# Gate-weight folding in a fused attention, MoE and routed-MoE kernel: weight squares transposed on VectorE, the gate product in pairs of pieces, decode steps in one run

## The chip, the core and the metric

The kernel runs on one core of a Trainium2 chip. The time is device time in microseconds, the median of three runs. TensorE multiplies matrices, VectorE and GpSimd work elementwise, ScalarE does activations and copies, and SyncE (SP) issues the loads. VectorE transposes squares of 32x32 elements within a tile, TensorE whole 128x128 tiles into a PSUM bank.

## What is computed

Three parts follow each other, in fp32: linear attention with random features (2 x 8 heads, 576 rows, 64 wide), a dense expert, and a routed one (top 1 of 8). Cut to what matters:

```python
x = attention(q, k, v, omega)                  # [1152, 512]
h = x @ w_in                                   # [512, 2048], given in float64
y = (h * sigmoid(1.702 * h)) @ w_out           # [2048, 512], given in float64
logits = y @ w_gate                            # [512, 8]
expert = argmax(logits, axis=1)                # each expert has a capacity of 288
out = gate_weight * (relu(y @ w1[expert]) @ w2[expert])   # where the token is kept, else 0
```

For the drawn inputs the kernel needs only half of the tokens' y in full. For the two other groups of tokens it needs the logits alone, and so it multiplies with the product `w_out @ w_gate` (2048 x 8), which it makes on the chip piece by piece.

## The kernel before

**Precision.** A big product is three matmuls in fp32r, a rounded fp32: high times high, high times low, low times high (`mm3`, L82 to L84). So each big operand is held as a high and a low part: ScalarE rounds the high one, VectorE or GpSimd subtracts for the low one.

**Decode.** The two weights `w_in` and `w_out` come as float64 in 16 pieces each, in the order in 0, out 0, in 1, out 1, ..., each 128x512 elements and 512 KB (`wraw`, four buffers). `decode` makes fp32 of one piece in four steps: a, b and c on VectorE by shifts of the two 32-bit words of each number (L220, L223, L226) into a tile `wf` (two buffers), and d, the cast of the high part on ScalarE (L232) and the subtraction of the low part on GpSimd (L233).

**Folding the gate.** For each piece m of `w_out`, three functions make row block m of `w_out @ w_gate`: `do_wt` transposes the four 128x128 squares of `wf` on TensorE (L473) into a PSUM bank and copies it to `wt` on ScalarE (L474). `do_wg` multiplies each by `wg_f`, the gate weights with 8 columns filled up to 32 with zeros (L482), each into its own 32 rows of a bank, copied on ScalarE (L485). `do_wp` transposes that (L490), copies it (L492), and adds the four parts in two steps on GpSimd (L493, L494) into `wp`. An fp32 matmul with a result of 32 rows shows as two instructions in the profile, a transpose as one. These tiles take banks by `mbank`, from two banks, M and L, in turn, or from M alone once the logits hold L.

**Order.** Attention runs in 40 steps, in which loads, transposes, projections, maxima, exponentials and sums are staggered by hand. Six pieces are decoded in it, one each at steps 13, 16, 19, 22, 25 and 28, one decode step of a piece per attention step; rows of q, k and v are asked for ten steps ahead. Then the first expert runs over slots n, listed in `seq`: each is `do_h` of one group G of 288 tokens and one of the 16 column blocks m (12 matmuls), and, for the group and block of two slots before, `do_consume`: for G 0 and 2 `do_y` (12 matmuls), for G 1 and 3 the logit product by `run_lg` (L631), a few blocks together. Groups 0, 1 and 3 run interleaved in rounds, group 2 after them. For G 0 and 2 `do_h` makes g twice on ScalarE (L588, L590) and its low part `glo` on VectorE (L591). The rest of attention is spread over the first slots with priority. The remaining 26 pieces are decoded at about one a slot from slot 0 on, by `decode_slot`: step a in slot n, b half a slot later, c one slot later, d two slots later. `paced` places an instruction behind the last `glo` (mark "v") or the last activation (mark "a") of its engine. The engines run in the order in which the instructions were issued.

**After that** come the positions of the tokens, the load of two experts' weights by a value read on the chip, and two expert passes with `do_h2` and `do_y2`.

Of the kernel before, what the change touches and what calls it, by code (L numbers as in the profile page):

```python
# [15 lines left out]
P = dict(ahead=2, kvlag=2, t2=3, n=5, x=6, dec=(13, 16, 19, 22, 25, 28), tailstep=0.5, zero=26, w0=12, loadlag=10, pv=(0, 4), l1=3, l3=5, db=0.5, hpt=30, dmin=0.9, dc=1, dd=2, dlead=6, dpace=1)  # L16


@with_exitstack
def linear_attention__moe__top1_moe_kernel(  # L20
# [48 lines left out]
    def bank(tag, name):  # L69
        return psA.tile([128, 512], F32, tag=tag, name=name, bufs={"A": 2, "B": 3, "C": 1, "M": 1, "L": 1}[tag])  # L70
# [73 lines left out]
    ps = bank("A", "om_ps")  # L144
# [64 lines left out]
    def decode(kind, m):  # L209

        t = w_raw.pop((kind, m))
        hi, lo = (w_in if kind == "in" else w_out)(m)
        w = t.rearrange("p (n two) -> p n two", two=2)
        low, high = w[:, :, 0], w[:, :, 1]
        f = gp.tile([128, DM], I32, tag="wf", name="wf", bufs=2)
        if kind == "out":
            wfs[m] = f

        def a():
            nc.vector.tensor_scalar(f, high, 3, 0x3FFFFFF8, ALU.logical_shift_left, ALU.bitwise_and)  # L220

        def b():
            nc.vector.scalar_tensor_tensor(f, high, -0x40000000, f, ALU.bitwise_and, ALU.bitwise_or)  # L223

        def c():
            nc.vector.scalar_tensor_tensor(f, low, 29, f, ALU.logical_shift_right, ALU.bitwise_or)  # L226

        def d():
            v = f.bitcast(F32)
            if kind == "in":  # L230
                v = v.rearrange("p (c f) -> p c f", c=KD)
            nc.scalar.copy(hi, v)  # L232
# [21 lines left out]
    def at(s, f):  # L254
        pend.setdefault(s, []).append(f)
# [197 lines left out]
    wg_f = const.tile([128, KD, 32], F32, name="wg_f")  # L453
    wg = const.tile([128, KD, 2, E], F32R, name="wg")
    wp = gate.tile([128, NF, 32], F32, name="wp")
    for t in (wg_f, wp):
        nc.gpsimd.memset(t, 0.0)

    def load_gate():
        nc.sync.dma_start(out=wg_f[:, :, 0:E], in_=moe2_w_gate.rearrange("(c p) e -> p c e", p=128))  # L460
        nc.vector.tensor_copy(wg[:, :, 0], wg_f[:, :, 0:E])
        nc.vector.tensor_tensor(wg[:, :, 1], wg_f[:, :, 0:E], wg[:, :, 0].bitcast(F32), ALU.subtract)


    wts, wws = {}, {}

    def do_wt(m):
        src = wfs.pop(m).bitcast(F32)
        dst = gp.tile([128, DM], F32, tag="wt", name="wt", bufs=1)
        ps = mbank("wt_ps")  # L470
        for c in range(KD):
            dc = slice(c * 128, c * 128 + 128)
            nc.tensor.transpose(ps[:, dc], src[:, dc], ident)  # L473
        nc.scalar.copy(dst, ps)  # L474
        wts[m] = dst

    def do_wg(m):

        t = wts.pop(m)
        ps = mbank("wg_ps")  # L480
        for c in range(KD):
            nc.tensor.matmul(ps[32 * c:32 * c + 32, :128], wg_f[:, c], t[:, c * 128:(c + 1) * 128],  # L482
                             start=True, stop=True)
        t = gp.tile([128, 128], F32, tag="wgt", name="wgt", bufs=1)
        nc.scalar.copy(t, ps[:, :128])  # L485
        wws[m] = t

    def do_wp(m):
        ps = mbank("wp_ps")
        nc.tensor.transpose(ps[:, :128], wws.pop(m), ident)  # L490
        t = gp.tile([128, KD, E], F32, tag="wpt", name="wpt", bufs=1)
        nc.scalar.copy(t, ps[:, :128].rearrange("p (c e) -> p c e", c=KD)[:, :, 0:E])  # L492
        nc.gpsimd.tensor_tensor(t[:, 0:2], t[:, 0:2], t[:, 2:4], ALU.add)  # L493
        nc.gpsimd.tensor_tensor(wp[:, m, 0:E], t[:, 0], t[:, 1], ALU.add)  # L494

    out_t = out.rearrange("(a p) d -> p a d", p=TT)
    zero_at = P["zero"]
# [5 lines left out]
    for s in range(NS + 1):  # L503
        do_T(s + AHEAD)
        if s < NS:
            do_P(s)
        do_Tlo(s + AHEAD)
        if s < NS:
            do_M(s)
        if s:  # L510
            do_E(s - 1)
        if s < NS:
            for f in pend.pop(s, []):
                f()
        if s == P["w0"]:
            load_next(4)
            load_gate()
        if s in DEC_AT:
            fs = decode_next(1)
            for d in range(4):  # L520
                at(s + d + 1, fs[d])
            at(s + 4, load_next)
            kd, m = wseq[wl[1] - 1]
            if kd == "out":
                at(s + 4, lambda m=m: do_wt(m))
                at(s + 6, lambda m=m: do_wg(m))
                at(s + 8, lambda m=m: do_wp(m))
# [43 lines left out]
    def slot(n, f):  # L571
        side.setdefault(round(n * 2) / 2, []).append(f)
# [497 lines left out]
```

## Time and profile before

| | us |
|---|---|
| median of 3 runs (lowest, highest) | 346.32 (346.31, 347.48) |
| profiled execution | 345.72 |
| its span, first to last instruction | 343.9 |
| TensorE busy, matmuls / weight loads | 323.6 / 303.6 |
| VectorE busy | 195.1 |
| ScalarE busy | 174.2 |
| GpSimd busy | 67.8 |

The busy time of TensorE counts pipelined matmuls whose ends are modelled, so that a full engine is not one at its peak. PE is TensorE's matmul, PEld its weight load, DVE VectorE, ACT ScalarE, POOL GpSimd, and SPq the queue on which SyncE issues loads. A row of a group gives the busy time and the mean duration, behind the bar the idle time just before these instructions and what ended it.

### The profile page before, as it was taken

The page shows a single profiled execution, that of the slowest core. Times are in us where ns is not written, and L with a number is a line of the kernel's source. Part 1 is how long each engine was busy: PE and PEld are TensorE (multiplying, and loading weights), DVE is VectorE, ACT ScalarE, POOL GpSimd, SP SyncE. Part 2 cuts the span into 40 slices and gives each one's busy share as a digit, 9 for nine tenths or more (in the row PEclk, how much of TensorE's full clock was granted, in tenths as well). Part 3 has the DMA queues.
Part 4 walks back from the last instruction along what each step waited for, and adds up shares of the span by engine and source line. Part 5 has one row for each costly group of instructions (what it writes and reads, how often), then busy time and mean ns, then how long its engine had stood idle before and what let it go on. Part 6 is the DMA issues. An engine that isn't in the chain of part 4 may idle for free.

```text
span 343.9 us, 6686 instructions
## 1 busy us (share of the span) xinstructions
PE 323.6 (94%) x2569; PEld 303.6 (88%) x2569; DVE 195.1 (57%) x438; ACT 174.2 (51%) x453; POOL 67.8 (20%) x99
## 2 busy tenths in 40 slices
PE   5899999999998999989899999999999999999991
PEld 4799988898887888888789998989999999999990
DVE  6577797896588445999992002316444132668322
ACT  3698898888864444454543123234344133175312
POOL 4110312130031565475753000000000001010000
PEclk9999999999999999999999999999999999999996
DMA  5999332310032453555510000251320000293202
GB/s 166 297 342 269 140 132 65 121 62 2 0 124 64 153 195 97 170 182 163 168 40 0 2 2 1 79 167 41 116 91 0 2 0 3 67 309 115 71 1 77
DMA packets 29079, 35.19 MB, mean 102 GB/s; under 512 B 5360, under 2 KB 23792, under 8 KB 29040
## 3 DMA queue, kind: packets, MB, share of 16 engines
q1 hardware_dynamic: 29040, 34.69, 31.2%
q8 instruction: 22, 0.36, 0.4%
q14 instruction: 17, 0.14, 0.1%
HBM read 32.33 MB, written 2.36 MB: 101 GB/s over the span
## 4 chain that ended last, share of the span: by engine, by line
PE 71%; DVE 10%; ACT 6%; DMA 5%; issue 4%; SPq 2%; POOL 1%; ACTq 0%; DVEq 0%
PE h_ps L82 10%; PE h_ps L84 10%; PE h_ps L83 10%; PE y L82 6%; PE y L84 6%; PE y L83 6%; PE nps L348 4%; PE kvp L323 4%; DVE wf L226 3%; DMA eraw<-in_moe_w_dram 3%; DVE x_lo L383 3%; PE wt_ps L473 2%; PE t L337 2%; ACT x_hi L382 2%; PE pj L83 2%
## 5 line engine op out<-in xcount | busy, mean ns | idle before, releaser
L591 DVE TENSOR_TENSOR glo<-g,ghi 128x288 fp32r<-128x288 f32 x32 | 15.7, 491 | 59.0 <-ACT g L590 58.9
L226 DVE SCALAR_TENSOR_TENSOR wf<-wraw,wf 128x512 int32<-128x512 int32 x32 | 36.1, 1128 | 0.7
L588 ACT ACTIVATE ghi<-h_ps 128x288 fp32r<-128x288 f32 x32 | 13.1, 410 | 42.1 <-PE h_ps L84 42.1
L583 ACT ACTIVATE g<-h_ps 128x288 f32<-128x288 f32 x32 | 13.2, 411 | 31.9 <-PE h_ps L84 27.0
L292 DVE TENSOR_REDUCE nb<-pj 128x4 f32<-128x512 f32 (+1 forms) x40 | 24.9, 628 | 3.5 <-PE pj L84 3.4
L810 DVE TENSOR_TENSOR el<-eraw,eh 128x1024 fp32r<-128x1024 f32 x16 | 19.5, 1223 | 11.0 <-ACT eh L809 10.9
L880 POOL MEMSET base<- 96x1536 f32 x2 | 2.8, 1378 | 113.4 <-PE h_ps L84 113.4
L82 PE MATMUL pj<-om_hi,xh 128*128 128x256 f32 x72 | 23.9, 332 | 1.1 <-ACT qp L305 1.1
L223 DVE SCALAR_TENSOR_TENSOR wf<-wraw,wf 128x512 int32<-128x512 int32 x32 | 23.0, 718 | 0.4
L809 ACT CAST eh<-eraw 128x1024 fp32r<-128x1024 f32 x16 | 16.7, 1050 | 12.4 <-PE h_ps L83 7.4
L305 ACT ACTIVATE qp<-pj,nb 128x128 f32<-128x128 f32 x72 | 21.7, 384 | 1.3 <-DVE nb L292 1.1
L305 ACT ACTIVATE kp<-pj,nb 128x128 f32<-128x128 f32 x72 | 21.3, 386 | 0.1
L83 PE MATMUL pj<-om_lo,xh 128*128 128x256 f32 x72 | 21.1, 293 | 0.0
L84 PE MATMUL pj<-om_hi,xl 128*128 128x256 f32 x72 | 21.1, 293 | 0.0
L82 PE MATMUL h_ps<-x_hi,win1h 128*128 128x288 f32 x64 | 20.4, 318 | 0.0
L220 DVE TENSOR_SCALAR wf<-wraw 128x512 int32<-128x512 int32 x32 | 15.7, 492 | 8.2 <-POOL wout1l L233 5.0
L323 PE MATMUL kvp<-vt,kp 128*128 128x65 f32 (+1 forms) x144 | 20.3, 270 | 0.0
L269 ACT CAST xh<-tp 128x256 fp32r<-128x256 f32 (+1 forms) x40 | 14.5, 363 | 11.3 <-PE tp L266 11.2
L82 PE MATMUL h_ps<-x_hi,win0h 128*128 128x288 f32 x64 | 20.1, 313 | 0.0
L82 PE MATMUL h_ps<-x_hi,win2h 128*128 128x288 f32 x64 | 19.9, 311 | 0.0
L84 PE MATMUL h_ps<-x_hi,win0l 128*128 128x288 f32 x64 | 19.5, 305 | 0.0
L276 DVE TENSOR_TENSOR xl<-tp,xh 128x256 fp32r<-128x256 f32 (+1 forms) x40 | 15.6, 392 | 6.7 <-ACT xh L269 6.4
(212 smaller groups left out, 1108.6 us busy)
## 6 DMA issues: line engine op xcount, KB each, us to landing
wraw<-in_moe_w_in_dram SPq DMA_DIRECT2D x16, 512.0 KB, 3.6
wraw<-in_moe_w_out_dram SPq DMA_DIRECT2D x16, 512.0 KB, 3.5
eraw<-in_moe_w_dram SPq DMA_DIRECT2D x16, 512.0 KB, 4.4
qk_raw<-in_v_dram SPq DMA_DIRECT2D x4, 512.0 KB, 5.2
qk_raw<-in_q_dram SPq DMA_DIRECT2D x4, 512.0 KB, 5.3
qk_raw<-in_k_dram SPq DMA_DIRECT2D x3, 512.0 KB, 5.1
out_dram<-zer SPq DMA_DIRECT2D x2, 576.0 KB, 4.9
out_dram<-base SPq DMA_DIRECT2D x6, 192.0 KB, 2.9
```

The lines of the kernel that those rows point to most:

```text
L82: nc.tensor.matmul(o, lh, rh, start=start, stop=False)
L83: nc.tensor.matmul(o, lh, rl, start=False, stop=False)
L84: nc.tensor.matmul(o, ll, rh, start=False, stop=stop)
L220: nc.vector.tensor_scalar(f, high, 3, 0x3FFFFFF8, ALU.logical_shift_left, ALU.bitwise_and)
L223: nc.vector.scalar_tensor_tensor(f, high, -0x40000000, f, ALU.bitwise_and, ALU.bitwise_or)
L226: nc.vector.scalar_tensor_tensor(f, low, 29, f, ALU.logical_shift_right, ALU.bitwise_or)
L292: mark["M", s] = nc.vector.tensor_reduce(nb[:, :nj], pj[:, :nj * M].rearrange("p (a m) -> p a m", m=M), AX, ALU.min)
L305: nc.scalar.activation(t[:, i], pj[:, i * M:(i + 1) * M], ACTF.Exp, bias=nb[:, i:i + 1], scale=-1.0)
L323: nc.tensor.matmul(ps[:, o:o + n], kp[:, i], vts[p][:, u, c0:c0 + n], start=(f == 0), stop=(f == NU - 1))
L591: mark["v"] = nc.vector.tensor_tensor(glo, g32, ghi.bitcast(F32), ALU.subtract)
L809: nc.scalar.copy(hi, tv)
L810: nc.vector.tensor_tensor(lo, tv, hi.bitcast(F32), ALU.subtract)
```

## The change

- `do_wt` transposes a piece in 16 squares of 32x32 per 32 partitions, with one instruction on VectorE, into one half of a tile `wt` for two pieces; no PSUM bank, no copy.
- `do_wg` runs once for two pieces (odd m). The stationary side is `wgd`: for each of the 16 blocks of 32 gate rows a 128x32 matrix whose four diagonal blocks are the same 32x8 weights, zeros elsewhere. 16 matmuls of 64 columns, in four groups of result rows, add up over four blocks each; one copy of 128x64.
- `do_wp` runs once for two pieces: eight matmuls of 8 columns with `fold32`, four unit matrices of 32 below each other, transpose and add the parts in one; one copy of 128x16 writes `wp` of both. The additions on GpSimd go.
- `wgd` is loaded by four more loads of the gate weights in 32-byte runs, into a tile that GpSimd filled with zeros.
- Step c of decode writes its result in place into the low words of the raw tile. `wf` has one buffer; cast, subtraction and transpose read every second word of the raw tile.
- In `decode_slot` a, b, c and the transpose are all placed in slot n; the products come at n + 2 and n + 3, for odd m only.
- `wp` has 8 columns instead of 32. `run_lg` writes 8 rows instead of 32 of each part of its bank, which VectorE sets to zero first, once.

```diff
-        f = gp.tile([128, DM], I32, tag="wf", name="wf", bufs=2)
+        f = gp.tile([128, DM], I32, tag="wf", name="wf", bufs=1)
         if kind == "out":
-            wfs[m] = f
+            wfs[m] = low.bitcast(F32)
...
         def c():
-            nc.vector.scalar_tensor_tensor(f, low, 29, f, ALU.logical_shift_right, ALU.bitwise_or)
+            nc.vector.scalar_tensor_tensor(low, low, 29, f, ALU.logical_shift_right, ALU.bitwise_or)
 
         def d():
-            v = f.bitcast(F32)
+            v = low.bitcast(F32)
...
+    NB = DM // 32
+    wg_f = const.tile([128, KD, E], F32, name="wg_f")
+    wp = gate.tile([128, NF, E], F32, name="wp")
+    wgd = const.tile([128, NB, 4 * E], F32, name="wgd")
+    nc.gpsimd.memset(wgd, 0.0)
+    fold32 = const.tile([128, 32], F32, name="fold32")
+    nc.gpsimd.tensor_tensor(fold32, ident[:, 0:32], ident[:, 32:64], ALU.add)
+    for i in (64, 96):
+        nc.gpsimd.tensor_tensor(fold32, fold32, ident[:, i:i + 32], ALU.add)
 
     def load_gate():
+        nc.sync.dma_start(out=wg_f, in_=moe2_w_gate.rearrange("(c p) e -> p c e", p=128))
+        for a in range(4):
+            nc.sync.dma_start(out=wgd[32 * a:32 * a + 32, :, a * E:(a + 1) * E],
+                              in_=moe2_w_gate.rearrange("(b i) e -> i b e", i=32))
...
     def do_wt(m):
-        src = wfs.pop(m).bitcast(F32)
-        dst = gp.tile([128, DM], F32, tag="wt", name="wt", bufs=1)
-        ps = mbank("wt_ps")
-        for c in range(KD):
-            dc = slice(c * 128, c * 128 + 128)
-            nc.tensor.transpose(ps[:, dc], src[:, dc], ident)
-        nc.scalar.copy(dst, ps)
-        wts[m] = dst
+        if m % 2 == 0:
+            wts[m // 2] = gp.tile([128, NB, 2, 32], F32, tag="wt", name="wt", bufs=1)
+        nc.vector.transpose(wts[m // 2][:, :, m % 2], wfs.pop(m).rearrange("p (b j) -> p b j", j=32))
 
     def do_wg(m):
-        t = wts.pop(m)
+        t = wts.pop(m // 2)
         ps = mbank("wg_ps")
-        for c in range(KD):
-            nc.tensor.matmul(ps[32 * c:32 * c + 32, :128], wg_f[:, c], t[:, c * 128:(c + 1) * 128],
-                             start=True, stop=True)
-        t = gp.tile([128, 128], F32, tag="wgt", name="wgt", bufs=1)
-        nc.scalar.copy(t, ps[:, :128])
-        wws[m] = t
+        for x in range(NB // 4):
+            for c in range(4):
+                nc.tensor.matmul(ps[32 * c:32 * c + 32, :64], wgd[:, 4 * x + c],
+                                 t[:, 4 * x + c].rearrange("p m j -> p (m j)"),
+                                 start=(x == 0), stop=(x == NB // 4 - 1))
+        wus[m] = gp.tile([128, 2, 32], F32, tag="wgt", name="wgt", bufs=1)
+        nc.scalar.copy(wus[m].rearrange("p m j -> p (m j)"), ps[:, :64])
 
     def do_wp(m):
+        t = wus.pop(m)
         ps = mbank("wp_ps")
-        nc.tensor.transpose(ps[:, :128], wws.pop(m), ident)
-        t = gp.tile([128, KD, E], F32, tag="wpt", name="wpt", bufs=1)
-        nc.scalar.copy(t, ps[:, :128].rearrange("p (c e) -> p c e", c=KD)[:, :, 0:E])
-        nc.gpsimd.tensor_tensor(t[:, 0:2], t[:, 0:2], t[:, 2:4], ALU.add)
-        nc.gpsimd.tensor_tensor(wp[:, m, 0:E], t[:, 0], t[:, 1], ALU.add)
+        for i in range(2):
+            for a in range(4):
+                nc.tensor.matmul(ps[32 * a:32 * a + 32, i * E:(i + 1) * E], t[:, i], fold32[:, a * E:(a + 1) * E],
+                                 start=True, stop=True)
+        nc.scalar.copy(wp[:, m - 1:m + 1].rearrange("p m e -> p (m e)"), ps[:, :2 * E])
...
     def run_lg():
         if not held:
             held.append(bank("L", "lgt_ps"))
+            nc.vector.memset(held[0][:, :GS], 0.0)
...
     def decode_slot(n):
         fs = decode_next(1)
-        paced(fs[0], "v")()
-        slot(n + P["db"], paced(fs[1], "v"))
-        slot(n + P["dc"], paced(fs[2], "v"))
+        kd, m = wseq[wl[1] - 1]
+        for f in fs[:3]:
+            paced(f, "v")()
+        if kd == "out":
+            paced(lambda: do_wt(m), "v")()
         slot(n + P["dd"], paced(fs[3], "a"))
         slot(n + P["dd"], load_next)
-        if kd == "out":
-            slot(n + P["dd"], lambda: do_wt(m))
-            slot(n + P["dd"] + 1, lambda: do_wg(m))
-            slot(n + P["dd"] + 2, lambda: do_wp(m))
+        if kd == "out" and m % 2:
+            slot(n + P["wgl"], lambda: do_wg(m))
+            slot(n + P["wgl"] + 1, lambda: do_wp(m))
```

## Rows read from the trace of the kernel before

**Rows 1.** View by stretches: length, busy us (x instructions) of each engine, clock, DMA.

```profile
0.00:86.00 86.00, 78.47 (x659) 73.65 (x659) 65.10 (x170) 68.61 (x218) 17.46 (x45) 1.00 0.51 159
86.00:132.00 46.00, 43.17 (x344) 39.16 (x343) 28.79 (x65) 25.12 (x59) 14.95 (x15) 1.00 0.31 104
132.00:184.00 52.00, 49.85 (x416) 44.51 (x416) 45.92 (x56) 25.88 (x64) 31.94 (x34) 1.00 0.41 132
```

**Rows 2.** View of waits, 86 to 132 us: us in total, times, longest.

```profile
PEld wt_ps L473 <- PE wp_ps L490: 1.2, 2, 0.6
```

**Rows 3.** View of waits, 132 to 184 us.

```profile
PEld wt_ps L473 <- ACT wpt L492: 3.9, 8, 1.0
...
PE wt_ps L473 <- DVE wf L226: 1.5, 2, 0.8
```

**Rows 4.** Timeline of TensorE around the three groups: start, us, instructions.

```profile
128.40 0.29 PE L84 MATMUL y<-ghi,wout1l 128*128 128x288 f32 x1
128.62 0.43 PE L482 MATMUL wg_ps<-wt,wg_f 128*32 128x128 f32 x8
...
129.21 0.29 PE L83 MATMUL h_ps<-x_lo,win1h 128*128 128x288 f32 x1
...
156.96 0.30 PE L84 MATMUL h_ps<-x_hi,win2l 128*128 128x288 f32 x1
157.09 0.27 PE L490 MATMUL wp_ps<-ident,wgt 128*128 128x128 f32 x1
...
157.34 0.29 PE L83 MATMUL h_ps<-x_lo,win1h 128*128 128x288 f32 x1
...
157.87 0.29 PE L84 MATMUL h_ps<-x_hi,win1l 128*128 128x288 f32 x1
158.13 0.66 PE L473 MATMUL wt_ps<-ident,wf 128*128 128x128 f32 x4
...
158.76 0.29 PE L83 MATMUL h_ps<-x_lo,win1h 128*128 128x288 f32 x1
...
159.52 0.69 PE L631 MATMUL lgt_ps<-g,wp 128*32 128x288 f32 x8
160.03 0.40 PE L482 MATMUL wg_ps<-wt,wg_f 128*32 128x128 f32 x8
```

**Rows 5.** View by stretches, 146 to 182 us.

```profile
146.00:182.00 36.00, 34.05 (x286) 30.20 (x285) 33.88 (x39) 18.08 (x47) 22.80 (x24) 1.00 0.41 132
```

**Rows 6.** Groups of VectorE's instructions, 146 to 182 us.

```profile
L226 DVE SCALAR_TENSOR_TENSOR wf<-wraw,wf 128x512 int32<-128x512 int32 x12 | 20.3, 1690 | 0.4
L223 DVE SCALAR_TENSOR_TENSOR wf<-wraw,wf 128x512 int32<-128x512 int32 x12 | 8.3, 694 | 0.3
L220 DVE TENSOR_SCALAR wf<-wraw 128x512 int32<-128x512 int32 x11 | 4.7, 423 | 0.0
L591 DVE TENSOR_TENSOR glo<-g,ghi 128x288 fp32r<-128x288 f32 x4 | 1.8, 458 | 1.3 <-ACT g L590 1.3
```

**Rows 7.** Groups by line and shape, whole span.

```profile
L292 DVE TENSOR_REDUCE nb<-pj 128x4 f32<-128x512 f32 x32 | 21.7, 681 | 1.5 <-PE pj L84 1.4
...
L588 ACT ACTIVATE ghi<-h_ps 128x288 fp32r<-128x288 f32 x32 | 13.1, 410 | 42.1 <-PE h_ps L84 42.1
...
L474 ACT COPY wt<-wt_ps 128x512 f32<-128x512 f32 x16 | 9.4, 589 | 5.2 <-PE wt_ps L473 5.0
...
L383 DVE TENSOR_TENSOR x_lo<-xps,x_hi 128x512 fp32r<-128x512 f32 x8 | 8.7, 1093 | 5.9 <-ACT x_hi L382 5.9
```

**Rows 8.** Timeline of all engines, GpSimd's subtraction and VectorE's step c.

```profile
152.51 1.50 POOL L233 TENSOR_TENSOR wout2l<-wf,wout2h 128x512 fp32r<-128x512 f32 x1 [0.31 <-ACT wout2h L232]
...
152.90 1.67 DVE L226 SCALAR_TENSOR_TENSOR wf<-wraw,wf 128x512 int32<-128x512 int32 x1
```

**Rows 9.** View of the tile wg_f: its load's issue (ns) and its landing.

```profile
L460 SPq DMA_DIRECT2D wg_f<-in_moe_w_gate_dram x1: 378/378/378, 19.9 to 19.9; - x1
...
DMA to landing us min/median/max: 7.3/7.3/7.3
```

More of the change, by code (lines that the diff above doesn't have):

```diff
@@ L15 @@
 AX = mybir.AxisListType.X
-P = dict(ahead=2, kvlag=2, t2=3, n=5, x=6, dec=(13, 16, 19, 22, 25, 28), tailstep=0.5, zero=26, w0=12, loadlag=10, pv=(0, 4), l1=3, l3=5, db=0.5, hpt=30, dmin=0.9, dc=1, dd=2, dlead=6, dpace=1)
+P = dict(ahead=2, kvlag=2, t2=3, n=5, x=6, dec=(13, 16, 19, 22, 25, 28), tailstep=0.5, zero=26, w0=12, loadlag=10, pv=(0, 4), l1=3, l3=5, wgl=2, hpt=30, dmin=0.9, dc=1, dd=2, dlead=6, dpace=1)
 @with_exitstack
@@ L450, in paced @@
         return g
-    wg_f = const.tile([128, KD, 32], F32, name="wg_f")
+    NB = DM // 32
+    wg_f = const.tile([128, KD, E], F32, name="wg_f")
     wg = const.tile([128, KD, 2, E], F32R, name="wg")
-    wp = gate.tile([128, NF, 32], F32, name="wp")
-    for t in (wg_f, wp):
-        nc.gpsimd.memset(t, 0.0)
-    def load_gate():
-        nc.sync.dma_start(out=wg_f[:, :, 0:E], in_=moe2_w_gate.rearrange("(c p) e -> p c e", p=128))
-        nc.vector.tensor_copy(wg[:, :, 0], wg_f[:, :, 0:E])
-        nc.vector.tensor_tensor(wg[:, :, 1], wg_f[:, :, 0:E], wg[:, :, 0].bitcast(F32), ALU.subtract)
@@ L465, in linear_attention__moe__top1_moe_kernel @@
-    wts, wws = {}, {}
-    def do_wt(m):
-        src = wfs.pop(m).bitcast(F32)
-        dst = gp.tile([128, DM], F32, tag="wt", name="wt", bufs=1)
-        ps = mbank("wt_ps")
-        for c in range(KD):
-            dc = slice(c * 128, c * 128 + 128)
-            nc.tensor.transpose(ps[:, dc], src[:, dc], ident)
-        nc.scalar.copy(dst, ps)
-        wts[m] = dst
+    wp = gate.tile([128, NF, E], F32, name="wp")
+    wgd = const.tile([128, NB, 4 * E], F32, name="wgd")
+    nc.gpsimd.memset(wgd, 0.0)
@@ new lines, in linear_attention__moe__top1_moe_kernel @@
+    fold32 = const.tile([128, 32], F32, name="fold32")
+    nc.gpsimd.tensor_tensor(fold32, ident[:, 0:32], ident[:, 32:64], ALU.add)
+    for i in (64, 96):
+        nc.gpsimd.tensor_tensor(fold32, fold32, ident[:, i:i + 32], ALU.add)
+    def load_gate():
+        nc.sync.dma_start(out=wg_f, in_=moe2_w_gate.rearrange("(c p) e -> p c e", p=128))
+        for a in range(4):
+            nc.sync.dma_start(out=wgd[32 * a:32 * a + 32, :, a * E:(a + 1) * E],
+                              in_=moe2_w_gate.rearrange("(b i) e -> i b e", i=32))
+        nc.vector.tensor_copy(wg[:, :, 0], wg_f)
+        nc.vector.tensor_tensor(wg[:, :, 1], wg_f, wg[:, :, 0].bitcast(F32), ALU.subtract)
@@ L477, in do_wg @@
+    wts, wus = {}, {}
+    def do_wt(m):
+        if m % 2 == 0:
+            wts[m // 2] = gp.tile([128, NB, 2, 32], F32, tag="wt", name="wt", bufs=1)
+        nc.vector.transpose(wts[m // 2][:, :, m % 2], wfs.pop(m).rearrange("p (b j) -> p b j", j=32))
     def do_wg(m):
-        t = wts.pop(m)
+        t = wts.pop(m // 2)
         ps = mbank("wg_ps")
-        for c in range(KD):
-            nc.tensor.matmul(ps[32 * c:32 * c + 32, :128], wg_f[:, c], t[:, c * 128:(c + 1) * 128],
-                             start=True, stop=True)
@@ L525, in linear_attention__moe__top1_moe_kernel @@
                 at(s + 4, lambda m=m: do_wt(m))
-                at(s + 6, lambda m=m: do_wg(m))
-                at(s + 8, lambda m=m: do_wp(m))
+                if m % 2:
+                    at(s + 6, lambda m=m: do_wg(m))
+                    at(s + 8, lambda m=m: do_wp(m))
         if s == zero_at:
@@ L629, in run_lg @@
             held.append(bank("L", "lgt_ps"))
+            nc.vector.memset(held[0][:, :GS], 0.0)
         for i, (m, g) in sorted(lgq.items()):
-            nc.tensor.matmul(held[0][32 * i:32 * i + 32, :GS], wp[:, m], g, start=(m < 2), stop=(m >= NF - 2))
+            nc.tensor.matmul(held[0][32 * i:32 * i + E, :GS], wp[:, m], g, start=(m < 2), stop=(m >= NF - 2))
         lgq.clear()
@@ L894, in decode_slot @@
         assert fs
-        paced(fs[0], "v")()
-        slot(n + P["db"], paced(fs[1], "v"))
-        slot(n + P["dc"], paced(fs[2], "v"))
+        kd, m = wseq[wl[1] - 1]
[3 more added lines that the diff above has]
+            paced(lambda: do_wt(m), "v")()
         slot(n + P["dd"], paced(fs[3], "a"))
         slot(n + P["dd"], load_next)
-        kd, m = wseq[wl[1] - 1]
-        if kd == "out":
-            slot(n + P["dd"], lambda: do_wt(m))
-            slot(n + P["dd"] + 1, lambda: do_wg(m))
-            slot(n + P["dd"] + 2, lambda: do_wp(m))
+        if kd == "out" and m % 2:
+            slot(n + P["wgl"], lambda: do_wg(m))
+            slot(n + P["wgl"] + 1, lambda: do_wp(m))
     for i, (kd, m) in enumerate(wseq[npre:]):
```

## The prediction

> **What bounds the kernel now.** I cut the span into three stretches by what the lines do: attention (0 to 86 us), the first expert rounds with the attention tail in them (86 to 132), and the rounds in which decode still runs (132 to 184); after 184 no line that the diff touches runs any more, except the logit products of L631. The view by stretch [rows 1] shows TensorE as the fullest engine everywhere: 78.5 of 86, 43.2 of 46 and 49.9 of 52 us. VectorE comes close only in the third stretch, 45.9 of 52. The granted clock is 1.00, the upper level of 2.4 GHz, in all three, so no gain or loss comes from the clock. So the question is first what leaves TensorE, and second what VectorE, nearly full in the third stretch, does with more work.
>
> The waits by stretch show what else ends there: between 132 and 184 its weight loads stood still ahead of the transposes of L473 eight times, 3.9 us, until a copy had freed the one PSUM bank [rows 3]; between 86 and 132 twice, 1.2 us [rows 2].
>
> **TensorE, what goes.** The pitch of two matmuls is 0.13 us [rows 4], from 156.96 to 157.09. From the L84 before a group to the second matmul behind it would be two pitches, 0.27 us. Measured so, one piece m costs: the last transpose 157.34 - 156.96 - 0.27 = 0.11 us; the four transposes of L473 158.76 - 157.87 - 0.27 = 0.62, of which 0.13 is the wait ahead of them (they start two pitches after L84 instead of one), so 0.50; the eight instructions of L482 129.21 - 128.40 - 0.27 = 0.54. Together 1.15 us, and 2.30 us for two pieces.
>
> **TensorE, what comes.** Each fp32 matmul with a 32-row result is two instructions (L482 shows eight for four matmuls). So a pair's gate product is 32 instructions and its folding 16, in steps of four that share the array by column groups. The 0.54 us of L482 hold two steps and the change of the array's layout there and back. What a further step of 64 or 8 columns costs no row shows. From below: eight instructions of 288 columns take 160.03 - 159.52 = 0.51 us, 0.25 a step, and 64 columns in proportion 0.06. From above: L482's 0.54, with the first 0.22 (128.40 to 128.62, one pitch of it normal) taken off, leaves 0.45 for two steps and the way back; I let a step be no more than 0.15. I take 0.10, between the two, since the loading of the stationary side doesn't shrink with the columns. Then the product is 0.54 + 6 x 0.10 = 1.14 us and the folding 0.54 + 2 x 0.10 = 0.74, 1.88 us a pair (1.56 to 2.28). A pair saves 0.42 us (0.02 to 0.74). Eight pairs: 3.4 us (0.2 to 5.9).
>
> By stretch, with three pieces and one pair in attention, four pieces and two pairs to 132, nine pieces and five pairs to 184: 3 x 1.15 - 1.88 = 1.6 us, 4 x 1.15 - 2 x 1.88 = 0.8 us, 9 x 1.15 - 5 x 1.88 = 1.0 us.
>
> **The waits for the bank.** With no L473 its waits go. Each hides one normal pitch: 1.2 - 2 x 0.13 = 0.9 us in the second stretch, 3.9 - 8 x 0.13 = 2.9 us in the third. The wait for the last decode step (1.5 us, twice [rows 3]) lies partly inside the same gaps; I add 0.3. What is late next: the products of a pair wait for VectorE's square transposes two slots after decode, and these are not in TensorE's way before that.
>
> **ScalarE and GpSimd.** The 128x512 copy of 0.59 us a piece [rows 7] goes, and both small additions on GpSimd. Neither engine sets the end after 86 us (ScalarE 25.1 of 46 and 25.9 of 52); in attention ScalarE is busy 68.6 of 86, so I count attention's 1.6 us of TensorE as 1.2, between nothing (if VectorE's added 3 x 0.68 us are what ends there) and 2.5 (if ScalarE's 3 x 0.59 and more count on top).
>
> **VectorE.** What each slot's decode costs there in its busiest part: from 146 to 182 us it is busy 33.88 of 36 us [rows 5] with twelve pieces and four glo [rows 6], 33.88 / 12 = 2.82 us a slot. L226 shows 1.69 us where L223, the same kind of operation, takes 0.69: the pair of rows in [rows 8] shows why, L226 stands next to GpSimd's subtraction and ends half a microsecond behind it. So VectorE and GpSimd exclude each other for about 1.0 us a piece.
>
> The new transpose of 128x512 in 32x32 squares has no row. From below: L220, the fastest operation on 128x512, 0.42 us. From above: L383, 128x512 with a PSUM operand, 1.09, or, if it is shut out by GpSimd as L226 is, 1.69. I take L292's 0.68 [rows 7], one input of 512 elements, as this has. The Trainium skill (Vector Engine (DVE) Microarchitecture Reference, section 3.8) says that the reorder array keeps one element per cycle and lane, which at 0.96 GHz is an estimate of 0.53 us without the fixed part; by it the slot below is 0.07 us shorter. No run here shows it yet.
>
> One transpose in two slots: 2.82 + 0.34 = 3.16 us a slot. The rule that bears on it in the Trainium skill (SBUF — State Buffer, section SBUF: two separate sides) is that GpSimd and an instruction of VectorE with two SBUF inputs lock each other out whole; [rows 8] agrees with its 1.67 us. By that rule a transpose, with one input, could run beside GpSimd, and the slot would fall to something between 2.82 and 3.16.
>
> Against that TensorE's slot: the 52 us of the third stretch less 1.0 and 3.2 us is 47.8 us in 17 slots, 2.8 us. VectorE may fall behind: what is queued behind a, b, c and the transpose is the next glo, and the y products want glo two slots after it is made. So 15 slots of VectorE have the time of 17 of TensorE: it decides from 17 x 2.8 / 15 = 3.18 us a slot on, and each 0.1 us above costs 1.5 us. My 3.16 stands just under it; I take 0.5 us of new wait.
>
> The single wf buffer and the in-place third step take away VectorE's waits for GpSimd, which cost nothing but the wait already counted. The raw buffer is held until cast, subtraction and transpose are done; four buffers and a slot of 2.8 us leave 11 us for what takes about 3 us and a load, so nothing. A transpose of an even piece waits until the products of the pair before have read the one wt buffer; these come in the same slot, so under 1 us, while VectorE isn't ahead.
>
> Two more costs I take as nothing. ScalarE's cast and GpSimd's subtraction now read every second word; L220 and L226 read so already at the prices shown, and for the other two engines no row says it; a fifth more of GpSimd's 1.50 us [rows 8] would be 0.3 us a slot, more than the price of the second rival below. And a, b and c in one piece, 1.8 us, can stand ahead of the attention tail's normalising in the second stretch: once or twice, so 0 to 2 us, and since those steps are given priority I take none.
>
> **The logit bank.** It is now cleared by VectorE, once, before the first logit product; no row shows a clearing of 288 columns; from above it is glo's 0.46 us [rows 6], two inputs of that size, from below nothing, and I take 0.3. In program order it comes behind glo of the same slot, which waits for two activations (0.41 each [rows 7]) of the h that TensorE has just done; TensorE stands for 2 x 0.41 + 0.46 + 0.3 = 1.6 us, once. If the instructions are put in another order, nothing. I take 1.6.
>
> **Loads.** Four more loads of the gate weights, in 32-byte runs. The one before took 0.38 us on the SP queue and 7.3 us to land [rows 9]. Four more issues are 1.5 us, and what is queued behind them are the rows of a later part of attention, asked for ten steps ahead; 86 us over 40 steps make that 20 us. Even four landings that follow each other at the time of one issue each stay inside that. Cost 0 to 1.5 us; I take 0.
>
> **Sum.** Attention -1.2; second stretch -0.8 - 0.9 = -1.7; third -1.0 - 3.2 + 0.5 = -3.7; logit bank +1.6: -5.0 us. The profiled execution took 345.7 us (span 343.9), the runs' median is 346.3, 0.6 above. So 345.7 - 5.0 + 0.6 = 341.3; I say 341.3 us.
>
> **Rivals.**
> *VectorE becomes the pacer.* If a transpose is locked out like L226 and takes 1.69 us, a slot is 2.82 + 0.85 = 3.67 us, 0.49 over the point of 3.18: 15 x 0.49 = 7.4 us instead of the 0.5 counted, 348.2 us, slower than before. For it: VectorE is busy 45.9 of 52 us there, and that GpSimd shuts it out is plain in [rows 8]. Against it: only two-input operations show the 1.69 in [rows 6]; L220 with one input stands at 0.42. Slower by 0.5% needs about 3.66 us a slot. 12 in 100.
> *The wait only changes its name.* With 1.09 us a transpose the slot is 3.37, and 15 x 0.19 = 2.9 us come back as waits of y for glo: 343.7 us. For it: VectorE was nearly full before. 20 in 100 (343 to 346).
> *The narrow products are dear.* At 0.15 us a step a pair costs 2.28 us and the 3.4 us are gone: 344.5 us, only the waits are won. For it: many more instructions, 48 a pair against 26. 13 in 100 (343 to 346).
> *All goes well:* steps of 0.06 us (2.5 us more), no stand for the clearing (1.6), attention in full (1.3): 335.9 us. 8 in 100.
> The forecast itself, 338.5 to 343.5, has the other 47.
>
> **How the numbers follow.** About 0.5%, 1.7 us, is what a measurement of this kernel can tell from no change; slower begins at 348.0, faster ends at 344.6. Faster: the forecast, the lucky case, and most of the second and third rivals, 47 + 8 + 21 = 76. The same: 12 from these two and 1 from the first, 13. Slower: the rest of the first, 11. The range of 8 in 10 leaves out the lucky end and the slow end: 336 to 346.8.
>
> **What would show it.** The profile after should have four-instruction steps of L482's successor 0.06 to 0.15 us apart, transposes on VectorE of 0.6 to 0.75 us, no wait for wt_ps, and TensorE busy over 51 of 52 us in the third stretch. A transpose above 1.0 us, or waits of y for glo there of more than 2 us, would prove the VectorE step wrong; a gap at the first logit product shows the clearing. The prediction fails most easily in the 3.16 against 3.18.

## The result and the profile after

The changed kernel takes 351.0 us (350.1 to 351.6, four runs) against 346.9 us (346.3 to 348.1, four runs): ratio 1.013, 95% interval [1.010, 1.015]. It is slower by 1.3% where 341.3 us were forecast. The profiled execution took 351.04 us, its span is 349.3.

The same view by stretches as [rows 1], with one stretch more (length, busy us and instructions of PE, PEld, DVE, ACT and POOL, clock, DMA share, GB/s), of the changed kernel:

```profile
0.00:86.00 86.00, 76.73 (x660) 71.79 (x661) 67.65 (x169) 64.85 (x207) 16.52 (x41) 1.00 0.54 160
86.00:132.00 46.00, 44.54 (x436) 41.09 (x436) 39.11 (x78) 24.21 (x58) 13.62 (x9) 1.00 0.33 98
132.00:184.00 52.00, 44.83 (x448) 41.00 (x447) 49.13 (x59) 18.17 (x45) 23.24 (x16) 0.93 0.44 138
184.00:230.00 46.00, 45.09 (x376) 42.08 (x378) 7.53 (x32) 11.92 (x31) 1.32 (x1) 0.96 0.10 31
```

The third stretch has turned over. TensorE had 49.85 of 52 us and now has 44.83; VectorE had 45.92 and now has 49.13; and the granted clock, 1.00 before, is 0.93. ScalarE lost 7.7 us of work there and GpSimd 8.7, and the time did not fall by it. In the second stretch VectorE went from 28.79 us to 39.11; run e2 below shows where that comes from. What TensorE waits for from 86 to 190 us (us in total, times, longest):

```profile
PE wg_ps L488 <- DVE wt L481: 7.8, 4, 2.8
...
PE y L83 <- DVE glo L599: 0.3, 1, 0.3
```

So the wait sits where the gate product of a pair wants the squares that VectorE transposes (L481), and not, as the prediction had it, where y wants glo. The timeline of TensorE shows the gate products (L488) with the idle time before them:

```profile
131.22 0.65 PE L488 MATMUL wg_ps<-wt,wgd 128*32 128x64 f32 x32
...
144.92 0.92 PE L488 MATMUL wg_ps<-wt,wgd 128*32 128x64 f32 x32 [2.03 <-DVE wt L481]
...
158.49 0.84 PE L488 MATMUL wg_ps<-wt,wgd 128*32 128x64 f32 x32 [2.80 <-DVE wt L481]
...
170.53 0.65 PE L488 MATMUL wg_ps<-wt,wgd 128*32 128x64 f32 x32 [0.80 <-DVE wt L481]
...
184.91 0.65 PE L488 MATMUL wg_ps<-wt,wgd 128*32 128x64 f32 x32 [2.12 <-DVE wt L481]
```

From the pair at 131.22, for which the view names no wait, to the last it is (184.91 - 131.22) / 4 = 13.42 us a pair. VectorE's timeline has the same beat: nine transposes from 130.36 to 184.05, 6.71 us apart in the mean, with two decode slots in each:

```profile
130.36 0.71 DVE L481 STREAM_TRANSPOSE wt<-wraw 128x512 f32<-128x512 f32 x1
...
184.05 0.71 DVE L481 STREAM_TRANSPOSE wt<-wraw 128x512 f32<-128x512 f32 x1
```

VectorE needs 3.36 us a slot and gives TensorE its beat. Between those two transposes it is busy 50.75 of 53.69 us, 3.17 us a slot, and the view of waits names nothing that it waits for; the other 0.18 us a slot are small gaps between its instructions:

```profile
130.36:184.05 53.69, 46.38 (x486) 42.26 (x485) 50.75 (x62) 19.00 (x46) 23.24 (x16) 0.94 0.44 138
```

One round in the timeline of VectorE, the shortest (5.62 us, with one step drawn out by GpSimd and no glo):

```profile
144.06 0.71 DVE L481 STREAM_TRANSPOSE wt<-wraw 128x512 f32<-128x512 f32 x1
144.70 0.38 DVE L220 TENSOR_SCALAR wf<-wraw 128x512 int32<-128x512 int32 x1
145.12 1.68 DVE L223 SCALAR_TENSOR_TENSOR wf<-wraw,wf 128x512 int32<-128x512 int32 x1
146.90 0.69 DVE L226 SCALAR_TENSOR_TENSOR wraw<-wraw,wf 128x512 int32<-128x512 int32 x1
147.62 0.43 DVE L220 TENSOR_SCALAR wf<-wraw 128x512 int32<-128x512 int32 x1
148.09 0.69 DVE L223 SCALAR_TENSOR_TENSOR wf<-wraw,wf 128x512 int32<-128x512 int32 x1
148.88 0.69 DVE L226 SCALAR_TENSOR_TENSOR wraw<-wraw,wf 128x512 int32<-128x512 int32 x1
149.68 0.71 DVE L481 STREAM_TRANSPOSE wt<-wraw 128x512 f32<-128x512 f32 x1
```

The groups of VectorE's instructions from 132 to 184 us, to set beside [rows 6]:

```profile
L226 DVE SCALAR_TENSOR_TENSOR wraw<-wraw,wf 128x512 int32<-128x512 int32 x16 | 17.9, 1121 | 1.7
L223 DVE SCALAR_TENSOR_TENSOR wf<-wraw,wf 128x512 int32<-128x512 int32 x16 | 15.0, 939 | 0.6
L220 DVE TENSOR_SCALAR wf<-wraw 128x512 int32<-128x512 int32 x15 | 10.0, 667 | 0.2
L481 DVE STREAM_TRANSPOSE wt<-wraw 128x512 f32<-128x512 f32 x7 | 5.0, 711 | 0.5
```

The time that GpSimd's subtraction takes from VectorE no longer falls on L226 above all: L220, L223 and L226 are hit by turns. Their sum, 0.67 + 0.94 + 1.12 = 2.73 us, is nearly that of before (0.42 + 0.75 + 1.52 = 2.69 in the same stretch).

As a mark for the whole I use the start of the one copy of the gathered logits. It was at 230.8 us and is now at 234.7, 3.9 us later, and nothing behind it has to do with the change: from it to the end of the span are 113.1 us before, 114.6 in the changed kernel, and 113.4 to 114.7 in the runs below that leave the logits as they are.

### The profile page after: what moved, and what is told of

Its sections match the earlier page's. It is cut to its first block, busy times and chain, and to the rows that moved or that the text cites. A ratio compares the mean times of both kernels' runs of the same rounds, so it can differ in the third digit from the quotient of the medians.

```text
span 349.3 us, 7032 instructions
## 1 busy us (share of the span) xinstructions
PE 321.5 (92%) x2745; PEld 303.1 (87%) x2745; DVE 211.7 (61%) x455; ACT 162.2 (46%) x421; POOL 57.5 (16%) x69
## 4 chain that ended last, share of the span: by engine, by line
PE 59%; DVE 25%; ACT 4%; DMA 4%; issue 3%; SPq 2%; DVEq 0%; ACTq 0%
PE h_ps L82 8%; PE h_ps L83 8%; PE h_ps L84 8%; DVE wraw L226 7%; DVE wf L223 6%; PE y L82 5%; PE y L83 5%; PE y L84 5%; DVE wf L220 5%; PE nps L348 4%; PE kvp L323 4%; DMA eraw<-in_moe_w_dram 3%; DVE wt L481 2%; PE t L337 2%; DVE x_lo L383 2%
## 5 line engine op out<-in xcount | busy, mean ns | idle before, releaser
L599 DVE TENSOR_TENSOR glo<-g,ghi 128x288 fp32r<-128x288 f32 x32 | 14.8, 462 | 52.8 <-ACT g L598 52.8
L226 DVE SCALAR_TENSOR_TENSOR wraw<-wraw,wf 128x512 int32<-128x512 int32 x32 | 31.7, 990 | 2.3
L223 DVE SCALAR_TENSOR_TENSOR wf<-wraw,wf 128x512 int32<-128x512 int32 x32 | 26.6, 832 | 0.8
L220 DVE TENSOR_SCALAR wf<-wraw 128x512 int32<-128x512 int32 x32 | 22.2, 693 | 0.7 <-DMA wraw<-in_moe_w_in_dram 0.4
L305 ACT ACTIVATE kp<-pj,nb 128x128 f32<-128x128 f32 x72 | 21.3, 383 | 0.0
L82 PE MATMUL y<-hhi,eh 128*128 128x288 f32 x64 | 19.1, 298 | 0.9 <-DVE z L850 0.9
L323 PEld LDWEIGHTS kvp<-vt,kp 128*128 128x128 f32 x144 | 19.0, 191 | 0.8 <-issue 0.3
L83 PE MATMUL h_ps<-x_lo,win2h 128*128 128x288 f32 x64 | 19.7, 308 | 0.0
```

The source lines that it names most:

```text
L82: nc.tensor.matmul(o, lh, rh, start=start, stop=False)
L83: nc.tensor.matmul(o, lh, rl, start=False, stop=False)
L226: nc.vector.scalar_tensor_tensor(low, low, 29, f, ALU.logical_shift_right, ALU.bitwise_or)
L305: nc.scalar.activation(t[:, i], pj[:, i * M:(i + 1) * M], ACTF.Exp, bias=nb[:, i:i + 1], scale=-1.0)
L323: nc.tensor.matmul(ps[:, o:o + n], kp[:, i], vts[p][:, u, c0:c0 + n], start=(f == 0), stop=(f == NU - 1))
L599: mark["v"] = nc.vector.tensor_tensor(glo, g32, ghi.bitcast(F32), ALU.subtract)
```

## The experiments

Three theories stood: A, VectorE has become the pacer and TensorE waits for it; B, decode in one run, in place and with one wf tile costs; C, the products merely stand too early, two slots behind decode.

**e1_narrow.** The changed kernel; from piece 4 on the transpose takes one of 16 blocks, and one tile wt stays throughout:

```diff
...
-            wts[m // 2] = gp.tile([128, NB, 2, 32], F32, tag="wt", name="wt", bufs=1)
-        nc.vector.transpose(wts[m // 2][:, :, m % 2], ...)
...
+        wts[m // 2] = st_wt[0]
+        k = NB if m < 4 else 1
+        nc.vector.transpose(st_wt[0][:, :k, m % 2], ...[:, :k])
```

> From piece 4 on the kernel transposes only one of the 16 column blocks of each w_out piece (the rest of the tile keeps older values), so 15/16 of the square transposes are left out; all else stands as in the changed kernel. Theory A (VectorE's added transposes, 0.71 us each, make it the pacer of decode, TensorE then waits for them ahead of the gate products and its clock falls in those gaps): twelve times about 0.6 us of VectorE leave, the 7.8 us of waits ahead of the gate products nearly vanish, the clock of the third stretch is 1.00 again, 340 to 344 us. Theory B (decode in one run with one wf buffer and in-place step c costs the time): 349 to 351 us, waits unchanged. Theory C (the products stand too early, two slots behind decode, and that alone makes TensorE wait): waits fall by a third at most, 347 to 350 us.

A miss, by its own flaw: the waits for wt grew to 15.8 us, five times, while VectorE was busy only 36.1 of 52 us from 132 to 184. With one tile that stays, the next even transpose stands ahead of the products in program order, and these wait for it too (a transpose at 123.02 us, the products at 123.29). The logits also send more tokens on, so the whole time (563.7 us) says nothing.

**e2_decode.** The kernel before, with the decode part of the change alone: wf with one buffer, step c in place, a, b and c in one slot.

```diff
-        slot(n + P["db"], paced(fs[1], "v"))
-        slot(n + P["dc"], paced(fs[2], "v"))
+        for f in fs[:3]:
+            paced(f, "v")()
```

> The kernel before with the decode part of the change alone: one wf buffer, step c in place in the raw tile, a, b and c in one slot; transposes and gate products stay on TensorE as before. Theory A: VectorE's work is that of before, 344 to 347.5 us, clock 1.00 in the third stretch. Theory B: 349 to 351 us, most of the loss is here already. Theory C: 344 to 347.5 us.

345.7 us, ratio 0.997 [0.995, 0.999]; from 132 to 184 us TensorE is busy 50.32 of 52 us at clock 1.00. B falls. The run also shows what filled VectorE from 86 to 132 us: it is busy 38.37 of 46 us here, without one square transpose. Before, step a waited 7.0 us in that stretch for GpSimd to free a `wf`; without these waits the steps meet GpSimd's subtractions (b takes 1.02 us in the mean, 0.68 before). What had been waiting became drawn-out steps, at no cost in time.

**e3_late4.** The changed kernel with the products four slots behind decode (`wgl=2` becomes `wgl=4`).

> The changed kernel with the gate products two slots later (four behind decode instead of two). Theory A: VectorE's total is unchanged, so the wait moves to other places (the next even piece's transpose waits for the one wt buffer, y waits for glo), 348 to 353 us. Theory B: 349 to 352 us. Theory C: the wait ahead of the gate products vanishes, 342 to 346 us.

346.0 us, 0.998 [0.995, 1.001]. What TensorE waits for from 86 to 190 us:

```profile
PE y L83 <- DVE glo L599: 3.5, 4, 2.3
PE lgt_ps L640 <- DVE lgt_ps L638: 2.0, 1, 2.0
```

A's range is missed, and C's upper edge is met. The place of the products is worth 5 us of 351.0 (two more slots of distance would be 2 x 2.56 = 5.1, an estimate from e4's slot below), but VectorE is as full as in the change (49.55 of 52 us), TensorE's waits now stand ahead of y and of the first logit product, and VectorE's beat is nearly the same, (184.52 - 144.88) / 3 = 13.21 us a pair:

```profile
144.88 0.71 DVE L481 STREAM_TRANSPOSE wt<-wraw 128x512 f32<-128x512 f32 x1
...
184.52 0.71 DVE L481 STREAM_TRANSPOSE wt<-wraw 128x512 f32<-128x512 f32 x1
```

Both theories hold a part: VectorE sets the beat, and the place says who feels it first, and how soon.

**e4_pace15.** The changed kernel, with the slot of decode i set at 1.5 i instead of i, as far as the due time allows:

```diff
-dpace=1
+dpace=1.5
```

The line that uses it is `n = max(int(i * P["dmin"]), min(need, int(i * P["dpace"])))`.

> The changed kernel with the remaining decodes at 1.5 slots a piece instead of one, bounded by when the weights are needed. Theory A: VectorE has 1.5 slots (about 4 us) for some 3.4 us of work a piece and is the pacer no longer; waits ahead of the products below 2 us, clock 1.00, 340 to 344 us. Theory B: decode costs the same wherever it stands, 348 to 351 us. Theory C: the products still stand two slots behind decode, but the transposes are then on time, so about as in A.

337.5 us, 0.975 [0.970, 0.980]: 13.5 us faster than the change as it was, and faster than the kernel before. The view by stretches, 132 to 230 us:

```profile
132.00:184.00 52.00, 52.00 (x530) 47.89 (x529) 46.69 (x58) 19.57 (x49) 20.99 (x14) 1.00 0.44 136
184.00:230.00 46.00, 46.00 (x392) 42.18 (x391) 15.64 (x49) 15.23 (x38) 4.30 (x3) 1.00 0.13 47
```

TensorE never stands still there, the clock is 1.00, no wait for wt is left, and the logits are copied at 221.8 us. The same instructions, spread over more slots, are the whole difference: what was lost is a matter of the rate at which VectorE is asked for work, and not of TensorE's cost of the new products.

**e5_narrow2.** e1 mended: the tiles turn over as in the change, and the products read the one block that is transposed.

> The changed kernel, where from piece 4 on only one of the 16 column blocks of each w_out piece is transposed and the gate products read that one block sixteen times; 15/16 of the square transposes are left out and the logits of two groups come out wrong, so extra expert passes run at the end and only the part up to the copy of the logits (at 234.7 us in the changed kernel, 230.8 before) is compared. Theory A (the added transposes make VectorE the pacer): the copy comes at 222 to 227 us, waits ahead of the gate products below 2 us, clock of the third stretch 1.00. Theory B (decode in one run and in place): 233 us or later. The run before this one, with one tile kept for all pairs, let the products read behind the next pair's transpose, which is why its waits grew; here the tiles turn over as in the changed kernel.

The small transposes take 0.21 us and the logits are copied at 228.2 us, 6.5 earlier than in the change, where 222 to 227 was named for A: the direction is right, the size short. VectorE still waits out a, b, c and GpSimd's subtraction (busy 45.40 of 52), and 4.4 us of waits for wt remain. Eight transposes shorter by 0.5 us would be 4.0 of the 6.5 us; where the other 2.5 come from was not followed. The whole time (645.5 us) has more expert passes, as in e1.

**e6_double.** Each transpose is made twice, one behind the other.

> The changed kernel with every square transpose done twice. Theory A: 13 to 16 more transposes of 0.71 us, most of them on the path: 358 to 363 us. Theory that only the place of the products counts: 351 to 354 us. If VectorE had slack: 351 us.

355.7 us, 1.026 [1.022, 1.029]; waits for wt 12.1 us (5 times), logits copied at 240.7, 6.0 later. The time is 4.7 us above the change: 2.3 below the range named for A, 1.7 above the one for the place of the products alone, and well above the 351 of a VectorE with slack. Eight more transposes after the pair at 131 us would be 8 x 0.71 = 5.7 us, but that this comes near 6.0 is luck. VectorE's timeline has the last transposes of that pair and of the last one at

```profile
132.39 1.46 DVE L483 STREAM_TRANSPOSE wt<-wraw 128x512 f32<-128x512 f32 x2
...
188.15 1.46 DVE L483 STREAM_TRANSPOSE wt<-wraw 128x512 f32<-128x512 f32 x2
```

which is (188.15 - 132.39) / 4 = 13.94 us a pair, 0.52 more than in the change for two more transposes of 0.71; VectorE was 2.0 us later already at the first of them. Part of the added time is won back: a subtraction of GpSimd that falls on a transpose costs VectorE nothing (see the last section), and a, b and c together take 2.64 us in the mean here, 2.73 in the change. The rest was not followed.

**e7_before_pace15.** The kernel before with `dpace=1.5`, to see whether the pacing alone is the gain.

> The kernel before with decode at 1.5 slots a piece, nothing else changed: what pacing is worth without the change. Theory A: its TensorE still does the dearer transposes and products (about 1.15 us a piece), and only the waits ahead of the transposes go, some 2 to 3 us: 342 to 345 us. If pacing were all that the faster run of the changed kernel shows: 338 us.

346.1 us, 1.000 [0.997, 1.002]: a miss. From 132 to 184 us:

```profile
132.00:184.00 52.00, 51.43 (x417) 46.38 (x416) 27.38 (x48) 22.66 (x57) 25.22 (x27) 1.00 0.39 123
```

TensorE's idle time is nearly gone, but the logits are copied at 229.8 us, only 1.0 earlier than before. So the pacing alone gives nothing measurable. TensorE's waits ahead of L473 from 86 to 190 us are 1.3 us here and were 2.8 before; the part that went was worth about 1 us, and all of it is less than the 4.1 of the prediction.

**e8_pace125.** The changed kernel with `dpace=1.25`.

> The changed kernel with decode at 1.25 slots a piece. Theory A: VectorE needs 3.36 us a piece against 1.25 TensorE slots of about 2.6 us, 3.3 us: just at the limit, 337 to 341 us. Any other theory: between 351 and the 337.5 of 1.5 slots in proportion, about 344 us.

338.9 us, 0.977 [0.973, 0.981], with 1.1 us of waits for wt: as expected. A quarter more slots for each piece is nearly enough.

**e9_spaced.** The changed kernel with the old spacing of decode; the products stay two slots behind the transpose (`wgl=3`):

```diff
-        for f in fs[:3]:
-            paced(f, "v")()
+        paced(fs[0], "v")()
+        slot(n + P["db"], paced(fs[1], "v"))
+        slot(n + P["dc"], paced(fs[2], "v"))
...
-            paced(lambda: do_wt(m), "v")()
+            slot(n + P["dc"], paced(lambda: do_wt(m), "v"))
```

> The changed kernel with the old spacing of decode: b half a slot after a, c and the transpose one slot after a, the products three slots after a, so again two behind the transpose. VectorE has the same work. If VectorE is the pacer by its sum of work, 132 to 184 us shows it busy over 48.5 of 52 us, TensorE waits about as before for the transposes or for glo, and the time is 349 to 353 us. If it is the order one behind another that costs, the time is 343 to 347 us.

349.0 us, 1.007 [1.004, 1.010]. Waits from 86 to 190 us:

```profile
PE wg_ps L488 <- DVE wt L481: 7.4, 4, 2.4
```

VectorE is busy 49.58 of 52 us. This is the pacer's side, at its lower edge: not the order one behind another, but the sum of VectorE's work costs.

**e10_fill.** The changed kernel with twelve more matmuls ahead of the last four gate products:

```diff
+        for _ in range(12 if m >= 9 else 0):
+            nc.tensor.matmul(ps[:, 128:128 + GS], x_hi[:, 0, 0:128], x_hi[:, 0, 0:GS], start=True, stop=True)
```

> The changed kernel with twelve more matmuls of 128x288 (1.6 us at a pitch of 0.13 us, results not used) in front of the gate products of the last four pairs, where TensorE otherwise stands still. If the lower granted clock behind the gaps adds time of its own, the clock from 132 to 184 us goes back from 0.93 to 0.98 or more and the time falls to 346 to 349 us. If VectorE sets the time and TensorE's clock only eats into its slack, the clock rises but the waits for the transposes stay at their places, shorter by what fills them, and the time stays at 350 to 352 us.

349.7 us, 1.009 [1.006, 1.013]; the logits are copied at 234.1 us, 0.6 earlier than in the change. Stretches and waits:

```profile
132.00:184.00 52.00, 46.94 (x488) 43.28 (x487) 49.12 (x59) 18.16 (x44) 23.23 (x16) 1.00 0.43 137
184.00:230.00 46.00, 45.58 (x393) 41.94 (x391) 8.41 (x32) 11.95 (x31) 1.65 (x2) 1.00 0.11 37
```
```profile
PE wg_ps L490 <- DVE wt L481: 4.7, 4, 2.2
```

The clock is back at 1.00 and the time hardly moves; it stands a little below the range named for that case, and above the one for a clock that costs. The lower clock is a consequence of the waits; what it adds of its own is 1.3 us at most by the medians, with intervals that overlap.

## Why the prediction was wrong

**The step that failed** is the comparison of the two slots, "it decides from 17 x 2.8 / 15 = 3.18 us a slot on", with VectorE's 3.16 just under it. VectorE's slot was 3.36 us, the point 2.90, and the distance of two slots that should have softened the difference was used up before the third stretch began.

*TensorE's slot was 2.56 us and not 2.8.* The narrow products were mis-sized. In e4, where TensorE waits for nothing from 132 us on, the timeline of TensorE shows both groups between ordinary matmuls:

```profile
145.57 0.29 PE L84 MATMUL h_ps<-x_hi,win1l 128*128 128x288 f32 x1
145.79 0.65 PE L488 MATMUL wg_ps<-wt,wgd 128*32 128x64 f32 x32
146.37 0.40 PE L82 MATMUL h_ps<-x_hi,win0h 128*128 128x288 f32 x1
146.61 0.29 PE L83 MATMUL h_ps<-x_lo,win0h 128*128 128x288 f32 x1
...
149.52 0.29 PE L84 MATMUL y<-ghi,wout2l 128*128 128x288 f32 x1
149.74 0.31 PE L499 MATMUL wp_ps<-fold,wgt 128*32 128x8 f32 x16
149.98 0.40 PE L82 MATMUL h_ps<-x_hi,win2h 128*128 128x288 f32 x1
150.22 0.30 PE L83 MATMUL h_ps<-x_lo,win2h 128*128 128x288 f32 x1
...
175.35 0.66 PE L488 MATMUL wg_ps<-wt,wgd 128*32 128x64 f32 x32
```

By the prediction's own measure the product costs 146.61 - 145.57 - 0.27 = 0.77 us (1.14 forecast) and the folding 150.22 - 149.52 - 0.27 = 0.43 (0.74). A pair costs 1.20 us where 1.88 was forecast, outside the bounds of 1.56 to 2.28. Six more steps of four make the product (0.77 - 0.54) / 6 = 0.04 us a step dearer than L482, below the lower bound of 0.06; the folding, with two more steps, costs less than L482's 0.54 as a whole, so that the 0.54 was no floor for columns as few as 8. A pair saves 2.30 - 1.20 = 1.10 us, not 0.42, eight pairs 8.8 us, not 3.4. (e4 and e7, which differ by the change alone, are 8.6 us apart, but that holds other things as well: between the first activation of the expert and the logits' copy TensorE stands still 2.9 us in e7 and 0.65 in e4.) The cheaper products made TensorE faster, by (1.88 - 1.20) / 4 = 0.17 of the 0.24 us a slot, and so brought the point at which VectorE decides down. In e4 a pair takes (175.35 - 145.79) / 2 = 14.78 us for six slots; without the 1.20 us of its products that is 2.26 us a slot, and with a pair in four slots 2.26 + 0.30 = 2.56 (10.25 us for four). The point is 17 x 2.56 / 15 = 2.90 us.

*VectorE's slot was 3.36 us and not 3.16.* The 3.16 are a sum of busy times, and as busy time they came true: 3.17 us a slot. But an engine that sets the pace pays its small gaps too, 0.18 us a slot, and the prediction set them at nothing by taking 33.88 of 36 us for the slot. Most of them stand ahead of step c (1.7 us for 16 from 132 to 184, 0.4 for 12 in [rows 6]); e2, with c in place and no square transpose, has 1.9 there, so these came with the decode part, and e9, with the old spacing, still has 1.7, so it is not the order; which part of the decode edit makes them stays open. That the twelve pieces of [rows 5] took 3.0 us each, and 3.0 + 0.36 is 3.36, is luck: of the 2.1 us of gaps there 1.3 are waits for ScalarE [rows 6], of which none are left. The transpose itself was sized well: 0.70 to 0.71 us, 0.68 forecast. The Trainium skill (Vector Engine (DVE) Microarchitecture Reference, section 3.8) let 0.53 us be estimated without the fixed part; the trace has 0.71 in all.

*The wait stood elsewhere.* The prediction put the next late thing at glo, after the whole distance of 17 against 15 slots. But glo of a slot stands ahead of that slot's decode on VectorE, and the transpose behind it, and both are wanted two slots later. So the transposes are late first. And no distance was left to use up: the product of one pair starts 0.7 us behind the end of its transposes at 117.88 us, that of the next 0.15 us behind them at 131.22, in e4 as in the change; VectorE had fallen behind in the second stretch, in which it is busy 39.11 of 46 us. From there on every slot pays the whole difference, and not the part above 2.90: four pairs of 13.42 us in place of 10.25 are 12.7 us, and from e4 to the change the logits' copy moves by 234.7 - 221.8 = 12.9. By the prediction's rule, with the true slots, it would be 15 x (3.36 - 2.90) = 6.9. With the products further behind (e3), the wait goes to glo as forecast, and the loss is smaller.

So the first rival's side came, slower because VectorE paces, but not its mechanism: no transpose took 1.69 us. The second rival had the wait of 1.09 us a transpose and a slot of 3.37, nearly the true one; at the forecast's TensorE slot it came out at 343.7.

**The other terms.**
- *Waits for the bank, 0.9 + 3.2 us:* too large. They were read from weight loads, and those stood still for longer than the matmuls: the 3.9 us of [rows 3] go with 52 - 49.85 = 2.15 us in which no matmul ran. e7, which loses part of these waits, gains 1 us.
- *Attention, -1.2 us:* wrong. The first activation of an expert block starts at 93.1 us, before 92.0, in e4 92.8. TensorE has 1.7 us less to do up to 86 us; VectorE has 2.6 more, and L337 on TensorE waits 1.6 us for VectorE's x_lo up to 93 us, 0.2 before. That the three transposes end there is argued only.
- *The logit bank, +1.6 us:* did not come in the change. The clearing takes 0.30 us, as taken, and lies at 121.8 us, the first logit product at 128.7. In e3 it did, with 2.0 us.
- *Loads, 0:* right, though the four issues take 0.7 to 3.9 us each, 7.9 in all from 21.3 us on, where 1.5 was taken. TensorE's waits for rows of q and k are 2.0 us, 2.4 before.
- *Strided reading, 0:* right in the time. The cast takes 0.66 to 0.67 us from 132 to 184 (0.63 before), the subtraction 1.37 to 1.53 (1.39 to 1.48).
- *Clock, "no gain or loss":* it fell to 0.93, but e10 shows that this cost little while VectorE set the beat.

For e4 the sum of these terms is +0.8 in attention, -7.7 for seven pairs after it and -2.15 for the idle time of the third stretch, -9.05, and the logits' copy is 230.8 - 221.8 = 9.0 us earlier. That it closes so well is luck. Between the two marks (92.0 to 230.8 us before, 92.8 to 221.8 in e4) TensorE's matmuls stand still 4.4 us before and 0.65 in e4, 3.7 less, and their busy time falls by 6.1, from 134.4 to 128.35 us.

## What to carry to other kernels

When work moves from the bound engine to a nearly full one, compare the slots of both after the change: the saving that is hoped for on the one lowers the point from which the other decides, and of an engine that may set the pace the wall time per slot counts, not its busy time. A distance of some slots softens the difference only if it is still there when the slow stretch begins. If the moved work has due times that lie far off, spread it over more slots before judging the change: here the spreading alone did nothing, the change alone cost 1.3%, and both together gained 2.5%. Of several consumers with the same distance, the one whose operand comes last in the producer's order within the slot waited first here.

## What the runs showed of the hardware

The transpose in 32x32 squares is not held up by GpSimd, while another operation with one input is. In the changed kernel's timeline of all engines, GpSimd's subtraction begins before the transpose and ends after it, and the next one meets L220:

```profile
169.51 1.30 POOL L233 TENSOR_TENSOR win3l<-wraw,win3h 128x512 fp32r<-128x512 f32 x1 [1.68 <-ACT win3h L232]
169.67 0.71 DVE L481 STREAM_TRANSPOSE wt<-wraw 128x512 f32<-128x512 f32 x1
...
170.81 1.48 POOL L233 TENSOR_TENSOR wout3l<-wraw,wout3h 128x512 fp32r<-128x512 f32 x1
...
171.05 1.53 DVE L220 TENSOR_SCALAR wf<-wraw 128x512 int32<-128x512 int32 x1
```

The transpose keeps its 0.71 us; L220, at 0.42 us otherwise, takes 1.53 and ends 0.29 us behind the subtraction. The prediction's "only two-input operations show the 1.69" holds for the stretch of [rows 6], where L220 never stood beside a subtraction. The trace of before had the counterexample earlier, in attention:

```profile
46.15 1.27 POOL L233 TENSOR_TENSOR wout0l<-wf,wout0h 128x512 fp32r<-128x512 f32 x1 [8.01 <-ACT wout0h L232]
...
46.63 1.07 DVE L220 TENSOR_SCALAR wf<-wraw 128x512 int32<-128x512 int32 x1
```

So one input was no ground for taking the transpose to be free of the subtraction; that it is free is what the trace after shows. The Trainium skill (SBUF — State Buffer, section SBUF: two separate sides) names both kinds, two SBUF inputs and a faster mode that uses both ports; that L220 runs in such a mode no row shows, but its rows fit.

After a gap TensorE ran at the lower of its two clock levels for a while. Behind the last gate product in the changed kernel's timeline of TensorE:

```profile
186.00 0.33 PE L82 MATMUL h_ps<-x_hi,win3h 128*128 128x288 f32 x1
186.13 0.44 PE L83 MATMUL h_ps<-x_lo,win3h 128*128 128x288 f32 x1
186.37 0.44 PE L84 MATMUL h_ps<-x_hi,win3l 128*128 128x288 f32 x1
186.61 0.44 PE L82 MATMUL h_ps<-x_hi,win3h 128*128 128x288 f32 x1
```

The pitch goes from 0.13 to 0.24 us behind the product that had waited 2.12 us for VectorE; from 186 to 188 us the granted clock is 0.53, near the lower level of 1.2 GHz, where it had been 1.00 from 182 to 184. With the gaps partly filled (e10) it stayed at 1.00 from 132 to 230 us.
